# Batch 1 of a two-level Strassen layer: seven block sums and differences at other places of VectorE's order

## The chip, the cores and the metric

The kernel runs on one core of a Trainium2 chip. The metric is the device time of one execution in microseconds (us); several executions are timed and the median is taken. A profile of one execution comes with it. In it PE is TensorE (PEld its weight loads), DVE VectorE, ACT ScalarE, and SP the queue from which all transfers are issued. L12 is line 12 of the kernel.

## What is computed

Cross-attention between 512 tokens and 32 state rows, for 8 batches of 8 heads, gives 544 rows of 512 columns per batch; a two-layer network with a quick GELU runs over all of them.

```python
scores = scale * x @ state^T                # (8, 8, 512, 32)
xread  = softmax(scores) @ state
scores2 = scale * state @ x^T               # (8, 8, 32, 512)
sread  = softmax(scores2) @ x
attn   = concat([xread, sread], axis=2)     # (8, 8, 544, 64)
x = attn.transpose(0, 2, 1, 3).reshape(-1, 512)
h = x @ w_in                                # w_in  512 x 2048
out = (h * sigmoid(1.702 * h)) @ w_out      # w_out 2048 x 512
```

## The kernel before

The second layer, `g @ w_out`, is done with Strassen's method in Winograd's form: seven products of half-size blocks instead of eight, with sums on both sides. From batch 1 on five or more of the seven are themselves done in this way, so that each consists of seven small products. For the weights' side, a block t with quarters b11, b12, b21, b22 needs three *small sums* (t1, t2, t4), which are kept in DRAM and loaded before they are used, and a *third* (b22 - b12), which overwrites the block's own quarter b12. These are made once, in batch 1 at the latest, by VectorE. After the third, the sums can no longer be made from the block.

```python
    def T_of(t, x0, x1):
        nc.vector.tensor_tensor(out=t, in0=x0, in1=x1, op=ALU.subtract)

    def low_sums(t, rooms):                   # three instructions of 128x512
        b11, b12, b21, b22 = halves_of(t)
        t1, t2, t4 = rooms
        return [(T_of, v) for v in ((t1, b12, b11), (t2, b22, t1), (t4, b21, t2))]

    def low_third(t):                         # one instruction of 128x4x128
        _, b12, _, b22 = halves_of(t)
        T_of(b12, b22, b12)
```

One product of seven small ones. x, y, z are banks of PSUM; `add` is VectorE's, `copy` ScalarE's. `at(i)` puts in, after the i-th small product, first the product's own further work (`own`) and then what hangs on the hook of that name: `P5.4` is the hook behind P5's fourth small product.

```python
    def strassen_low(left, right, bank, R, at):
        ...
        product(x, a11, b11, True)
        nc.scalar.copy(y, x)
        at(1)
        product(z, s1, t1, True)
        nc.scalar.copy(c22, z)
        at(2)
        product(y, s2, t2)
        nc.scalar.copy(c12, y)
        at(3)
        product(x, a12, b21)
        nc.scalar.copy(c11, x)
        at(4)
        product(y, a21, t3)        # t3 is the third
        add(c22, y, c22)           # L697
        at(5)
        product(z, s4, b22)
        add(c12, z, c12)           # L697
        at(6)
        product(y, a22, t4)        # writes y again
        nc.scalar.copy(c21, y)
        at(7)
```

The products of batch 1, in order (key is 1):

```python
        product(bank(0), A_of(0, 0), B11, "P1")         # batch 1: P1 and P2 in one piece
        nc.scalar.copy(k1, bank(0))
        ...
            for i in range(3):
                sums1[i]()
                hook(f"S1.{i}")
            third_of(S1)
            product(bank(1), A_of(0, 1), B21, "P2")     # hooks P2a and P2b after its halves
            tt(osb, bank(1), k1)
        out(0, 0, osb)
        ...
        hook("P2")
        ...                                             # s4, sums2, third_of(S2) in P5's at()
        o, h0, h1 = low_banks()                         # o is bank_o[1]
        strassen_low(left_of(S1, *r), (b11, t3, b21, b22, *low_b), [h0, h1, o], p5, at)   # P5: T1
        low_load(6, 1)                                  # B22's kept sums, for P3
        hook("P5")
        ...
        lowly("P6", left_of(S2, q1, q2, q4), T2, low_a, banks, k2, own6)
        low_load(3, 0)
        ...
        lowly("P3", left12, B22, low_b, [h0, h1, o], p3, own3)
        ...
        hook("run")                                     # here low4_load: T4's kept sums back
        ...
        lowly("P7", left3, T3, low_a, [o, h0, h1], k3, {k + 1: steps4[k : k + 1] for k in range(4)})
        ...
        lowly("P4", left4, T4, low_parts(a4["low4"]), [o, h1, h0], k1, ...)
```

T4's small sums are made in a tile with the tag xT, of which there is one buffer. Before that, batch 2's exponentials e2 lie there, from which four transfers to DRAM (`squares`) read. Their issue hangs on P2b.

```python
    def away(k):
        room = apool.tile([P, NPR, S], FP32, tag="xT", name=f"away_{k}")
        return room.rearrange("p j t -> p (j t)")[:, : 3 * FC]

    def T4_sum(i):
        if i == 0:
            away4.append(away(4))
        fn, args = low_sums(T4, low_parts(away4[0]))[i]
        fn(*args)
        if i == 2:
            low_keep(4, away4[0])             # to DRAM

    def eT_out(b):
        for j in range(NPR):
            src = e2_room[b][Ns * j : Ns * (j + 1), :NG].rearrange("n g (i q) -> n g i q", i=SCH)
            nc.sync.dma_start(squares[:, :, :, j].rearrange("i n g q -> n g i q"), src)
```

Into the same hooks goes the attention of batch 2: its scores (att_blocks, att_s_max) at P2a, `att_s_norm` and `x_max` at P6.1, `x_sub` at P6.2, and so on.

Of the kernel before, what the change touches and what calls it, by code (L numbers as in the profile page):

```python
# [20 lines left out]
def kernel(  # L21
# [85 lines left out]
    T2, T4 = T24[:, :, 0], T24[:, :, 1]  # L107
# [24 lines left out]
    def load_state(b):  # L132
        stn[b] = apool.tile([P, NG, D], FP32, tag="stn", name=f"stn_{b}", bufs=2)
        for g in range(NG):
            nc.sync.dma_start(stn[b][:, g], st_v[b, g])
# [16 lines left out]
    def load_x_squares(b):  # L152
        xsq[b] = xpool.tile([P, NPR, S], FP32, tag="xn", name=f"xsq_{b}")
        for g in range(NG):
            for k in range(D // Ns):
                o = D * g + Ns * k
                dst = xsq[b][o : o + Ns].rearrange("p j (t a) -> p j t a", a=Ns)
                for j in range(NPR):
                    nc.sync.dma_start(dst[:, j], x_sq[b, g, k][:, j])
# [478 lines left out]
    T3 = w_out[:, :HF, HN:]  # L638
# [12 lines left out]
    def low_keep(k, src):  # L651
        nc.sync.dma_start(outside[k], src)
# [21 lines left out]
    def low_sums(t, rooms):  # L674
# [5 lines that stand above are left out]
    def low_third(t):  # L680
        _, b12, _, b22 = halves_of(t)
        T_of(b12, b22, b12)
# [346 lines left out]
    def parts_x(b):  # L1029

        a = A[b]
        t1, t2, t3, t4 = ([t] for t in a["T"])
        r11, r21, r22 = [a["aT"][:, 0, :QT]], [a["aT"][:, 1, :QT]], [a["aT"][:, 1, QT:]]

        def left(u):
            c = u // 2
            lo, hi = a["M", c], a["M", 2 + c]
            return [lo[:, 0]], [lo[:, 1]], [hi[:, 0]], [hi[:, 1]], [a["S1"][:, c]], [a["S2"][:, c]], [a["S4"][:, c]]

        return left, (r11, r21, r22, t1, t2, t3, t4)  # L1040
# [230 lines left out]
    B11, B12, B21, B22 = (w_out[:, HF * i : HF * (i + 1), HN * k : HN * (k + 1)] for i in range(2) for k in range(2))  # L1271
# [18 lines left out]
    def out_of(b):  # L1290
        return lambda r, n: out_x[b, r, :, n].rearrange("r q n -> q r n")
# [28 lines left out]
    def turns_of(*lists):  # L1320

        for step in zip(*lists):
            for fn, args in step:
                fn(*args)
# [147 lines left out]
    for b in range(1, B):  # L1472
        if b == 2:

            turns_of(low_sums(B11, low_b))
            low_keep(0, turn_rooms[1])
            low_third(B11)
        if b > 1:
            beside = [(turns_of, ([*low_sums(B21, low_a), (low_keep, (1, turn_rooms[0])), (low_third, (B21,))],))]
            ahead = {"P1.1": [(up_strassen(b, S, *parts_x(b), A[b]["sums"], beside if b == 2 else ()), ())]}  # L1480
        else:
            ahead = {
                "P2b": [(low_made, (2, T2, 0)), (low_third, (T2,))],
                "P5.4": [(T4_sum, (0,))],
                "P5.6": [(T4_sum, (1,))],
                "P6.2": [(T4_sum, (2,))],
                "P6.4": [(low_third, (B22,))],
                "P3.4": [(low_third, (T3,))],
                "P7.3": [(low_third, (T4,))],
            }  # L1490
            for u in range(NU - 1):
                ahead[f"S1.{u}"] = [(s3, (1, u, S))]
        if b + 1 < B:
            hooks = hooks_next(b + 1)
        else:

            steps, left, right = sr_sums()
            order = (
                ("P5.6", 2), ("P6.1", 3), ("P6.3", 6), ("P6.4", 7), ("P7.5", 8), ("P7.6", 9), ("P4.1", 16, 17), ("P4.5", 18, 19),
            )  # L1500
            hooks = {name: [steps[i] for i in n] for name, *n in order}
            hooks["P3.7"] = [(low_third, (T1,))]
            beside = steps[10:16] + [(low_third, (t,)) for t in (B11, B21, T2, T3, T4, B22)]
            ahead["P2.1"] = [steps[i] for i in (0, 1)]
            ahead["P2.3"] = [steps[i] for i in (4, 5)]
        for name, first in ahead.items():
            hooks[name] = first + hooks.get(name, [])
        a4 = {}

        at = hooks.setdefault("run", [])  # L1510
        k = 3 if b + 1 < B else 0
        at[k:k] = [(low4_load, (a4,))]
        strassen_two(b, out_of(b), hooks, a4)
        if b + 2 < B:
            load_state(b + 2)
            load_x_squares(b + 2)
# [35 lines left out]
```

## Time and profile before

| | before |
|---|---|
| median of three runs | 700.7 us (699.64 to 701.02) |
| span of the profiled execution | 699.1 us |
| TensorE busy | 684.5 us (98%) |
| VectorE busy | 571.5 us (82%) |
| ScalarE busy | 321.0 us (46%) |
| bytes moved | 87.41 MB, mean 125 GB/s |
| mean granted clock of TensorE | 0.997 |
| batch 1's second layer in the span | about 147 to 204 us |

The busy share of an engine is an average over the whole span. A matmul counts as busy for as long as it takes, also when TensorE's clock is throttled, and so a slow stretch doesn't show as idle time. The time at which an instruction starts, and in brackets the idle time of its engine before it with the event that ended it, is read from the timeline.

### The profile page before, as it was taken

What the parts mean: (1) busy time and instruction counts of PE and PEld (TensorE: products, weight loads), DVE (VectorE), ACT (ScalarE), POOL (GpSimd) and SP (SyncE); (2) the same over time, 40 slices, a digit from 0 to 9 for tenths busy, and PEclk for the clock granted to TensorE, in tenths of its full rate; (3) what the DMA queues carried; (4) which work ended last, traced back from release to release, by engine and by line L of the source; (5) the groups of instructions that cost most, each with busy time, mean ns of one, the idle gap of its engine ahead of it and who ended that gap; (6) DMA issues with size and microseconds to landing.
All of it is one profiled execution on the core that took longest, in us unless ns stands there. A gap on an engine that the chain in (4) does not pass through costs nothing.

```text
span 699.1 us, 13774 instructions
## 1 busy us (share of the span) xinstructions
PE 684.5 (98%) x5359; PEld 579.6 (83%) x5359; DVE 571.5 (82%) x1210; ACT 321.0 (46%) x704; POOL 0.8 (0%) x8
## 2 busy tenths in 40 slices
PE   8989999998999999999999999999999999999996
PEld 3433587776998899889988999889988998999995
DVE  6999998998898889697969886988778895887540
ACT  5688843223337523654355434653376236422420
POOL 0000000000000000000000000000000000000000
PEclk9999999999999999999999999999999999999999
DMA  8921337056525374436551664157433740251001
GB/s 232 368 72 58 122 121 183 8 189 181 175 68 140 106 241 138 80 91 212 151 110 31 190 211 113 20 139 234 138 53 106 241 137 16 74 155 50 11 2 31
DMA packets 106321, 87.41 MB, mean 125 GB/s; under 512 B 64784, under 2 KB 85776, under 8 KB 106256
## 3 DMA queue, kind: packets, MB, share of 16 engines
q1 hardware_dynamic: 106256, 86.53, 42.6%
q8 instruction: 43, 0.70, 0.4%
q14 instruction: 22, 0.18, 0.1%
HBM read 68.94 MB, written 17.56 MB: 124 GB/s over the span
## 4 chain that ended last, share of the span: by engine, by line
PE 90%; ACT 4%; DVE 2%; DMA 2%; SPq 1%; issue 0%; DVEq 0%
PE low L692 26%; PE o L1104 15%; PE o L692 14%; PE upx L1104 6%; PE h L547 4%; PE o L1371 4%; PE M L329 4%; PE down L1371 3%; PE o L589 2%; PE upw L1104 2%; PE down_up L547 2%; PE o L741 1%; PE o L329 1%; PE warm L127 1%; PE upx_sr L1104 1%; PE sr L518 1%
## 5 line engine op out<-in xcount | busy, mean ns | idle before, releaser
L692 PE MATMUL low<-w_out,g 128*128 128x128 f32 x416 | 54.3, 276 | 0.0
L692 PEld LDWEIGHTS low<-w_out,g 128*128 128x128 f32 x416 | 50.5, 192 | 4.5 <-issue 4.2
L1104 PE MATMUL o<-ta,M 128*128 128x256 f32 x192 | 49.9, 382 | 0.0
L1104 PE MATMUL upx<-aT,M 128*128 128x256 f32 x192 | 49.3, 379 | 0.0
L692 PE MATMUL low<-low,g 128*128 128x128 f32 x336 | 43.7, 277 | 0.2 <-DVE later L697 0.2
L692 PEld LDWEIGHTS low<-low,g 128*128 128x128 f32 x336 | 40.7, 194 | 0.3 <-DVE later L697 0.3
L1104 PEld LDWEIGHTS o<-ta,M 128*128 128x128 f32 x192 | 35.5, 190 | 6.0 <-ACT g L1150 1.6
L1104 PEld LDWEIGHTS upx<-aT,M 128*128 128x128 f32 x192 | 36.0, 190 | 4.6
L476 ACT COPY M<-M 128x512 f32<-128x512 f32 x59 | 30.7, 595 | 16.9 <-PE M L329 16.9
L692 PE MATMUL low<-sums,later 128*128 128x128 f32 x280 | 36.7, 279 | 0.0
L1110 ACT ACTIVATE g<-o 128x512 f32<-128x512 f32 (+1 forms) x56 | 31.3, 559 | 10.5 <-PE o L1104 10.5
L692 PEld LDWEIGHTS low<-sums,later 128*128 128x128 f32 x280 | 34.4, 196 | 0.1
L329 PE MATMUL M<-w_in,stT 64*32 64x512 f32 x472 | 32.6, 595 | 0.0
L1104 PE MATMUL o<-ta,ms 128*128 128x256 f32 x120 | 30.8, 379 | 0.0
L547 PE MATMUL h<-aT,M 128*128 128x512 f32 x64 | 28.7, 599 | 1.4 <-ACT M L476 1.4
L1150 ACT COPY g<-o 128x512 f32<-128x512 f32 (+1 forms) x28 | 15.5, 554 | 25.4 <-PE o L1104 25.4
L547 PEld LDWEIGHTS h<-aT,M 128*128 128x128 f32 x64 | 11.8, 190 | 18.3 <-issue 12.0
L1110 ACT ACTIVATE g<-g 128x512 f32<-128x512 f32 (+1 forms) x28 | 16.8, 600 | 20.8 <-DVE g L1113 20.8
L227 ACT ACTIVATE low<-low,edge 128x512 f32<-128x512 int32 x30 | 21.6, 718 | 8.7 <-DVE low L216 8.6
L1104 PEld LDWEIGHTS o<-ta,ms 128*128 128x128 f32 x120 | 22.8, 190 | 3.1
L1104 PE MATMUL o<-aT,m 128*128 128x256 f32 x96 | 24.6, 379 | 0.0
L692 PE MATMUL low<-low,later 128*128 128x128 f32 x168 | 22.5, 281 | 1.9 <-DVE spare_M L697 1.9
(290 smaller groups left out, 1646.7 us busy)
## 6 DMA issues: line engine op xcount, KB each, us to landing
low<-low SPq DMA_DIRECT2D x108, 256.0 KB, 3.6
low<-low SPq DMA_DIRECT2D x11, 768.0 KB, 4.3
later<-in_moe_w_out_dram SPq DMA_DIRECT2D x16, 512.0 KB, 3.5
w_out<-in_moe_w_in_dram SPq DMA_DIRECT2D x12, 512.0 KB, 5.6
xsq<-in_x_dram SPq DMA_DIRECT2D x96, 64.0 KB, 2.3
xn<-in_x_dram SPq DMA_DIRECT2D x12, 512.0 KB, 4.2
out_dram<-osb SPq DMA_DIRECT2D x15, 256.0 KB, 2.2
out_dram<-later SPq DMA_DIRECT2D x14, 256.0 KB, 2.1
```

The costliest lines, as they stand in the source:

```text
L127: nc.tensor.matmul(ps, zeros[:, :P], zeros, start=True, stop=True)
L227: nc.scalar.activation(out=sc.bitcast(FP32), in_=sc, func=AF.Relu, bias=edge[0], scale=-8.0)
L329: nc.tensor.matmul(ps[g][st], A[b]["stT"][rows, st], rhs(rows, j), start=True, stop=True)
L476: nc.scalar.copy(m[:, g], ps[g])
L518: nc.tensor.matmul(ps[st, g], e, v, start=(c == 0), stop=(c == SCH - 1),)
L547: nc.tensor.matmul(hps, lhs[i], rhs[i], start=(i == 0), stop=(i == n - 1))
L589: nc.tensor.matmul(ps[:, r], lhs[f][:, P * r : P * (r + 1)], rhs[:, f], start=(first and r == 0 and f == 0), stop=(f == HF - 1), skip_grou ...
L692: nc.tensor.matmul(ps, lhs[f], rhs[:, f], start=(first and f == 0), stop=(f == QF - 1), skip_group_check=True)
L1104: nc.tensor.matmul(ps[:, k], lhs[i][:, o : o + P], rhs[i], start=(first and k == 0 and i == 0), stop=(i == n - 1), skip_group_check=True,)
L1110: nc.scalar.activation(out=dst, in_=src, func=AF.Gelu_apprx_sigmoid)
L1150: nc.scalar.copy(c12, Y(u))
L1371: nc.tensor.matmul(ps7[name][:, HN * r : HN * (r + 1)], lhs[:, P * r : P * (r + 1)], rhs, start=(i == 0 and r == 0), stop=(i == HF - 1), s ...
```

## The change

It takes the same seven VectorE instructions of batch 1 to other places of that engine's order: the three small sums of T4 from P5.4, P5.6 and P6.2 to P6.1, P6.2 and P6.3, and the thirds of B22, T2, T3 and T4 to earlier or later hooks. The order that the data demand is kept: each third after its block's sums and before the fifth small product that uses it. The aim is that T4's sums come at a point where their room is free, and that what stands in their old places waits for nothing.

```diff
             ahead = {
-                "P2b": [(low_made, (2, T2, 0)), (low_third, (T2,))],
-                "P5.4": [(T4_sum, (0,))],
-                "P5.6": [(T4_sum, (1,))],
-                "P6.2": [(T4_sum, (2,))],
-                "P6.4": [(low_third, (B22,))],
-                "P3.4": [(low_third, (T3,))],
-                "P7.3": [(low_third, (T4,))],
+                "P2a": [(low_third, (B22,))],
+                "P2b": [(low_made, (2, T2, 0))],
+                "P2": [(low_third, (T2,))],
+                "P5.4": [(low_third, (T3,))],
+                "P6.1": [(T4_sum, (0,))],
+                "P6.2": [(T4_sum, (1,))],
+                "P6.3": [(T4_sum, (2,))],
+                "P3.4": [(low_third, (T4,))],
             }
```

What is listed here runs ahead of the attention's steps on the same hook. `low_made` makes T2's three small sums and sends them to DRAM.

## The prediction

> **What bounds the kernel now.** I read the page first. Its busy shares say TensorE, and the slices say that it is nearly never idle:
>
> ```profile
> PE 684.5 (98%) x5359; PEld 579.6 (83%) x5359; DVE 571.5 (82%) x1210; ACT 321.0 (46%) x704; POOL 0.8 (0%) x8
> PE   8989999998999999999999999999999999999996
> PE 90%; ACT 4%; DVE 2%; DMA 2%; SPq 1%; issue 0%; DVEq 0%
> ```
>
> TensorE is 98% busy and carries 90% of the chain that ended last. No arithmetic is added or removed here, so the only time to be had is TensorE's remaining idle time, plus matmuls that count as busy but run slowly. I therefore looked at where the chain leaves TensorE inside the second-layer products of batch 1 (147 to 204 us, the only stretch whose order changes). The timeline of TensorE (start, length, tile, count, in brackets the idle time before and who ended it) has two stalls between 160 us and 190 us and one small one at 196 us:
>
> ```profile
> 165.95 1.16 PE L692 MATMUL o<-low,spare_M 128*128 128x128 f32 x8 [0.59 <-DVE osb L748]
> 169.63 1.06 PE L692 MATMUL o<-sums,spare_M 128*128 128x128 f32 x8
> 172.59 1.70 PE L692 MATMUL low<-low,later 128*128 128x128 f32 x8 [1.91 <-DVE spare_M L697]
> 174.08 1.92 PE L692 MATMUL low<-sums,later 128*128 128x128 f32 x8
> 175.79 1.37 PE L692 MATMUL low<-low,g 128*128 128x128 f32 x8
> 180.57 1.06 PE L692 MATMUL o<-low,later 128*128 128x128 f32 x8
> 196.66 1.16 PE L692 MATMUL low<-low,g 128*128 128x128 f32 x8 [0.16 <-DVE later L697]
> ```
>
> In the kernel's terms these rows are: P5's second, sixth and seventh small product, P6's first, second and seventh, and P7's seventh. P5.7 waits 1.91 us for VectorE's addition after P5.5. A small product normally starts 0.89 us after the one before (P6.3 177.00, P6.4 177.89, P6.5 178.79), but P5.7, P6.1 and P6.2 need 1.49, 1.71 and 1.21. The granted clock, in half-microsecond windows of TensorE (window, length, busy with count, clock, DMA share, GB/s), says why:
>
> ```profile
> 172.50:173.00 0.50, 0.41 (x3) 1.00 0.66 254
> 173.00:173.50 0.50, 0.50 (x5) 0.53 0.05 16
> ...
> 176.00:176.50 0.50, 0.50 (x4) 0.56 1.10 426
> 176.50:177.00 0.50, 0.50 (x7) 1.00 1.04 426
> ```
>
> The clock is halved for some 3.5 us after the stall. In 4 us windows over the first 236 us it is below 1.00 only here. The page's clock row shows 9 throughout, so the dip is easy to miss. The stall thus costs 1.91 us and then 4.57 us for 24 matmuls that take 2.68 us elsewhere in the chain, another 1.89 us.
>
> Why was VectorE late? Its timeline:
>
> ```profile
> 163.27 1.42 DVE L1274 TENSOR_TENSOR low<-sums,low 128x512 f32<-128x512 f32 x2 [0.46 <-DVE low L1274]
> 164.61 0.68 DVE L1274 TENSOR_TENSOR sums<-sums 128x512 f32<-128x512 f32 x1
> 165.21 0.68 DVE L748 TENSOR_TENSOR osb<-o,g 128x512 f32<-128x512 f32 x1
> 168.82 0.69 DVE L748 TENSOR_TENSOR g<-later,g 128x512 f32<-128x512 f32 x1
> 171.64 0.69 DVE L1274 TENSOR_TENSOR away<-sums 128x512 f32<-128x512 f32 x1 [2.14 <-DMA squares<-e]
> 172.25 0.28 DVE L697 TENSOR_TENSOR spare_M<-low,spare_M 128x128 f32<-128x128 f32 x1
> ```
>
> The first of T4's small sums (away<-sums) writes into the room from which the four transfers squares<-e still read. The chain has the last issued at 167.74 and 3.78 us to its landing, at 171.52. VectorE stands 2.14 us before it, and the addition that TensorE needs (spare_M, L697) is behind it in VectorE's order, although P5.5's result was ready at about 168.73 + 1.06 = 169.79. The earlier stall has the same form: the third of T2 (sums<-sums) stands ahead of the osb addition, which has to empty the bank that P5.2 writes.
>
> **What the Trainium skill says.** "TensorE: Matmul & The Clock Gate", "Architectural detail", states that VectorE's queue is strict first-in-first-out: what waits at its head holds all behind it. The trace agrees, with the 2.14 us. The same page, "What's actually happening", describes a clock gate that goes to half rate after a free-running window of about 3.4 us with too little activity, and needs as long a busy window to open again. Here the clock did fall to 0.50, and for about 3.5 us; but an idle stretch of 1.9 us was enough, so a window that is only partly idle can do it. An idle 1.45 us (at 36 us) did not: the clock there stays 1.00.
>
> **The change part by part.** A third or sum of 128x512 costs VectorE 0.60 us from start to start when work follows (164.61 to 165.21), a 128x128 addition 0.20 (172.25 to 172.45). All seven instructions (three sums of T4, four thirds) are kept and only change place. No engine but VectorE has its order changed.
>
> *Third of B22, from P6.4 to P2a.* It comes after third_of(S1), which starts at 158.03 and leaves VectorE idle 0.64 us until the score transposes at 159.35, which wait for TensorE. The third takes 158.63 to 159.23: free, within 0.1 us.
>
> *Third of T2, behind the osb addition.* P2's product ends at 160.75 + 3.72 = 164.47 and T2's last small sum ends at 163.27 + 1.42 = 164.69, so osb can start at about 164.65, not 165.21, and P5.2 at 165.35 instead of 165.95. TensorE gains 0.60 us for the moment. VectorE's later work is unmoved: both still end at 165.81.
>
> *T4's sums away from P5.4, third of T3 there.* VectorE reaches this place at 168.82 + 0.60 = 169.42 as before, but the third of T3 waits for nothing and ends its turn at 170.02. P5.5 will be ready (168.13 + 1.06 = 169.19), so the L697 addition runs 170.02 to 170.30, and P5.7 starts near 170.35 instead of 172.59. TensorE is free for it at 169.03 + 0.89 = 169.92, so a wait of about 0.4 us remains. *Gain at P5.7: 2.24 us.*
>
> *Clock.* With an idle stretch of about 0.4 us (0.59 at 165 and 0.7 at 10 to 13 us left the clock at 1.00) I expect no dip. Products follow at 0.893 us: P6.3 at 170.35 + 3 x 0.893 = 173.03 instead of 177.00, P6.5 at 174.82, P6.7 at 176.60 instead of 180.57. *Gain at P6.7: 3.97 us.*
>
> *T4's sums at P6.1, P6.2, P6.3.* VectorE: s4 at 170.22, the L697 addition after P5.6 at 170.82, s4 at 171.02, free at 171.62. The room comes free at 171.52, and the first sum started 0.12 us after that, 171.64. So it now stands there just when the transfers end: no wait to speak of. Then, with the starts of the trace before, 2.36 us to the place after the second spare_M sum of P6.2 (173.85 to 176.21, the same instructions): 174.01 for the second sum, x_sub 174.61, third sum 175.22, free at 175.82. P6.5 is ready 1.16 us after its start (178.79, addition 179.95), hence at 175.98. VectorE is there 0.16 us early, the addition ends at 176.27, and P6.7 can start on time at 176.60, with 0.33 us to spare.
>
> *Third of T4, from P7.3 to P3.4.* It takes the place of T3's third, so nothing moves until P7.3; from there VectorE has 0.60 us less before the addition that P7.7 waited 0.16 us for. That wait goes too: VectorE 196.66 - 3.97 - 0.60 = 192.09, TensorE 196.50 - 3.97 = 192.53. *Gain: 0.16 us.*
>
> Sum: 2.24 + (3.97 - 2.24) + 0.16 = 4.13 us. After 197 us TensorE's timeline shows no stall up to the last first-layer products that I looked at (285 us), and VectorE idles there now and again (1.92 us at 242, 2.03 at 255, both for TensorE), so the rest should move earlier as a block. 700.7 - 4.1 = 696.6 us.
>
> **Rivals.** *The wait moves to P6.5.* If the four transfers land later, or the first T4 sum pays for its four transfer waits one after the other, all beyond 0.33 us goes straight to P6.7. For: T4's sums now stand before that addition with no spare time, and DMA engines are 90% or more busy from 166 to 172.6. Against: the transfers' issue follows ScalarE's exponentials, which nothing here moves. A slip of 1 us gives 697.3. *The clock dips anyway.* The idle time would be about 0.4 us and the gate's windows run freely; then 1.9 us are lost again: 698.5. *VectorE becomes the bound.* From 181.96 to 196.41 it has no idle time, so a TensorE that gains can run into it. Against: its own waits of 2.14, 1.85 and 0.24 us go too, with 0.60 us of work taken out, 4.83 us in all, more than TensorE's 4.13; but a stumble in the middle could leave only half the gain: 698.6. *The gain is handed back later*, at a transfer that doesn't come earlier: 700.7. Against: x, the kept sums and the state are loaded when buffers come free, and these move along.
>
> **Range and chances.** 696.6 us, with 695.5 to 698.6 for 8 in 10: the low end is the sum with half a microsecond of further small waits gone and the runs' scatter (699.64 to 701.02), the high end one of the second or third rival in full. Over 2% would need 14 us either way, and a stretch with 2.7 us of stalls and 1.9 us of slow clock holds no such gain. Nothing new is put in that could cost as much. So 0.985 within 2%, 0.01 faster, 0.005 slower.
>
> **What would show it.** Right: P5.2 starts near 165.35 with hardly a wait; the addition before P5.7 runs at about 170.0 behind a third of T3 (w_out<-w_out); P5.7's wait is 0.3 to 0.6 us; clock 1.00 from 172 to 177; away<-sums first at 171.6; P6.7 at about 176.6; batch 2's first-layer products (upx) start at 203.9 - 4.1 = 199.8. Wrong: a TensorE wait at P6.5 to P6.7 on L697, a halved clock after P5.7, or a later stage of batch 2 that starts where it did before.

## The result and the profile after

The changed kernel takes 697.18 us (median of six, 696.78 to 697.51) against 700.59 us for the kernel before (six, 699.64 to 701.62): a ratio of 0.9952, 95% interval 0.9939 to 0.9964. A second comparison gave 697.01 us and 0.9949 (0.9935 to 0.9964). The change brings about half a percent; 696.6 us had been predicted.

The page of the changed kernel, busy times and the chain by engine:

```profile
PE 682.9 (98%) x5357; PEld 578.0 (83%) x5359; DVE 571.6 (82%) x1210; ACT 321.0 (46%) x704; POOL 0.8 (0%) x8
PE 90%; DVE 5%; DMA 2%; ACT 1%; SPq 0%; issue 0%; DVEq 0%
```

The work is the same (VectorE 571.6 us against 571.5). TensorE's busy time fell by 1.6 us although it does the same matmuls (two records of them are missing in this trace). That is the time of the halved clock: P5.7, P6.1 and P6.2 took 4.41 us before (172.59 to 177.00), and take 2.78 us here (170.38 to 173.16). TensorE's timeline, of the small products in the prediction P5.2, P5.6, P5.7, P6.7 and P7.7:

```profile
165.37 1.16 PE L692 MATMUL o<-low,spare_M 128*128 128x128 f32 x8
169.04 1.06 PE L692 MATMUL o<-sums,spare_M 128*128 128x128 f32 x8
170.38 1.16 PE L692 MATMUL low<-low,later 128*128 128x128 f32 x8 [0.28 <-DVE spare_M L697]
176.74 1.06 PE L692 MATMUL o<-low,later 128*128 128x128 f32 x8
192.51 1.06 PE L692 MATMUL low<-low,g 128*128 128x128 f32 x8
```

Of the three stalls of before (0.59, 1.91, 0.16 us) only one, at P5.7, is left, and it is 0.28 us. P6.7 starts 3.83 us earlier than before (180.57), P7.7 4.15 us (196.66). The granted clock in the stretch where it was halved (window, length, busy with count, clock, DMA share, GB/s):

```profile
173.00:174.00 1.00, 1.00 (x11) 1.00 0.75 244
174.00:175.00 1.00, 1.00 (x11) 1.00 1.02 367
```

And VectorE's timeline, with the same places as before:

```profile
162.47 0.68 DVE L1274 TENSOR_TENSOR low<-sums 128x512 f32<-128x512 f32 x1
163.25 1.42 DVE L1274 TENSOR_TENSOR low<-sums,low 128x512 f32<-128x512 f32 x2
164.62 0.69 DVE L748 TENSOR_TENSOR osb<-o,g 128x512 f32<-128x512 f32 x1
169.44 0.68 DVE L1274 TENSOR_TENSOR w_out<-w_out 128x512 f32<-128x512 f32 x1
170.04 0.28 DVE L697 TENSOR_TENSOR spare_M<-low,spare_M 128x128 f32<-128x128 f32 x1
171.64 0.69 DVE L1274 TENSOR_TENSOR away<-sums 128x512 f32<-128x512 f32 x1
```

The third of T3 (w_out) stands where the first T4 sum waited 2.14 us. The addition for P5.7 runs at 170.04 instead of 172.25, and the T4 sum comes at 171.64 without any wait. One row was not expected: T2's second small sum starts 0.78 us after the first, where it took 1.14 (162.13 to 163.27). The section on the thirds comes back to it.

### The profile page after: what moved, and what is told of

Its sections match the earlier page's. It is cut to its first block, busy times and chain, and to the rows that moved or that the text cites. A ratio compares the mean times of both kernels' runs of the same rounds, so it can differ in the third digit from the quotient of the medians.

```text
span 695.1 us, 13772 instructions
## 1 busy us (share of the span) xinstructions
PE 682.9 (98%) x5357; PEld 578.0 (83%) x5359; DVE 571.6 (82%) x1210; ACT 321.0 (46%) x704; POOL 0.8 (0%) x8
## 4 chain that ended last, share of the span: by engine, by line
PE 90%; DVE 5%; DMA 2%; ACT 1%; SPq 0%; issue 0%; DVEq 0%
PE low L692 27%; PE o L1104 15%; PE o L692 15%; PE upx L1104 6%; PE h L547 4%; PE o L1371 4%; PE M L329 4%; PE down L1371 3%; PE o L589 2%; PE upw L1104 2%; PE down_up L547 2%; PE o L741 1%; PE sr L518 1%; PE upx_sr L1104 1%; DMA out_dram<-osb_sr 1%; PE o L329 1%
## 5 line engine op out<-in xcount | busy, mean ns | idle before, releaser
L692 PEld LDWEIGHTS o<-w_out,g 128*128 128x128 f32 x160 | 19.4, 192 | 5.0 <-issue 5.0
```

The source lines that it names most:

```text
L692: nc.tensor.matmul(ps, lhs[f], rhs[:, f], start=(first and f == 0), stop=(f == QF - 1), skip_group_check=True)
```

## The experiments

Each run is compared with the kernel before on the same chip. All 85 executions of the kernel before that stood beside the experiments fall into two groups by their mean granted clock: 37 under 0.998 with a median of 701.57 us (700.97 to 702.59), and 48 at 0.998 or more with 699.86 us (699.25 to 700.86). I call them "with the dip" and "without". Both profiles taken of the kernel before are of the first kind.

### T4's sums alone, and the thirds alone

The theory was that the first T4 sum, at the head of VectorE's order, waits for its room and holds up the addition that TensorE needs. The rival: VectorE is the bound, and the thirds' places carry a good part. Each half of the change was run without the other. The first:

```diff
-                "P5.4": [(T4_sum, (0,))],
-                "P5.6": [(T4_sum, (1,))],
-                "P6.2": [(T4_sum, (2,))],
+                "P6.1": [(T4_sum, (0,))],
+                "P6.2": [(T4_sum, (1,))],
+                "P6.3": [(T4_sum, (2,))],
```

> Only T4's three small sums move (P5.4, P5.6, P6.2 to P6.1, P6.2, P6.3); the four thirds stay where they were before. Theory A (the gain comes from the first T4 sum no longer standing at VectorE's head, waiting for the four transfers out of its room, with a TensorE stall of 1.91 us and a halved clock of 1.89 us behind it): P5.2 still waits near 0.6 us and starts at 165.95; the addition before P5.7 runs at about 169.5; P5.7 starts at its free time, 170.5, with hardly a wait; clock 1.00 from 172 to 177; P6.7 at 176.8 (before 180.57, after 176.74); P7.7 keeps its wait of about 0.2 us; about 3.7 us less than before, 696.9 us. Rival B (the thirds' places matter as much, since VectorE is the bound): P6.5's addition comes late behind the third of B22 and P6.7 waits 0.5 us or more; gain 2 to 3 us, 698 us.

Measured: 697.76 us against 701.1, ratio 0.9956 (0.9941 to 0.9971), no execution with the dip. TensorE's timeline of this run, P5.2, P5.7, P6.7 and P7.7:

```profile
165.88 1.16 PE L692 MATMUL o<-low,spare_M 128*128 128x128 f32 x8 [0.58 <-DVE osb L748]
170.45 1.06 PE L692 MATMUL low<-low,later 128*128 128x128 f32 x8
176.70 1.15 PE L692 MATMUL o<-low,later 128*128 128x128 f32 x8
192.89 1.16 PE L692 MATMUL low<-low,g 128*128 128x128 f32 x8 [0.15 <-DVE later L697]
```

The stall of 0.58 us before P5.2 and that of 0.15 us before P7.7 are still there, the long one is gone, and P6.7 is as early as in the whole change (176.74). So the T4 sums carry nearly all of it: by P7.7 3.77 us of the 4.15 us of the whole change. The third of T2 gains 0.5 us at P5.2, nearly all of which the third of T3 at P5.4 gives back at P5.7 (170.45 here, 170.38 in the whole change). The starts came as expected; the time is 0.9 us above the expected 696.9 us, which, like the prediction, took the halved clock as lost in every execution.

The second half:

```diff
-                "P2b": [(low_made, (2, T2, 0)), (low_third, (T2,))],
-                "P5.4": [(T4_sum, (0,))],
+                "P2a": [(low_third, (B22,))],
+                "P2b": [(low_made, (2, T2, 0))],
+                "P2": [(low_third, (T2,))],
+                "P5.4": [(low_third, (T3,)), (T4_sum, (0,))],
...
-                "P6.4": [(low_third, (B22,))],
-                "P3.4": [(low_third, (T3,))],
-                "P7.3": [(low_third, (T4,))],
+                "P3.4": [(low_third, (T4,))],
```

> Only the four thirds move, as in the changed kernel (the third of T3 stands at P5.4 ahead of the first T4 sum); T4's sums keep their old places P5.4, P5.6, P6.2. Theory A: P5.2 starts 0.6 us earlier, at 165.4, and hands it back: the first T4 sum still waits for the transfers until 171.6, P5.7 still starts at about 172.6 after an idle 2.5 us, the clock is halved again for about 3.5 us, P6.7 at 180.6; only the 0.16 us at P7.7 goes; 700.4 us, no difference that shows. Rival B (the thirds carry a good part of the gain): 697 to 699 us.

Measured: 698.85 us, ratio 0.9969 (0.996 to 0.9977), with no dip in 15 executions. My theory had expected 700.4 us, and missed by 1.5 us; the time is within the 697 to 699 us of the rival. VectorE's timeline:

```profile
169.67 0.68 DVE L1274 TENSOR_TENSOR w_out<-w_out 128x512 f32<-128x512 f32 x1
170.97 0.69 DVE L1274 TENSOR_TENSOR away<-sums 128x512 f32<-128x512 f32 x1 [0.62 <-DMA squares<-e]
171.57 0.28 DVE L697 TENSOR_TENSOR spare_M<-low,spare_M 128x128 f32<-128x128 f32 x1
```

The wait is still there as the theory had it, but the four transfers landed 2.81 us after the last was issued, by the chain, and not 3.78 us. The room came free earlier, and the thirds have something to do with it. That is not the rival's reason, a bound by VectorE; three runs in the section on the thirds look for the cause.

### Another room for T4's sums

If it is the wait for the room and not the work at P5.4, another room in the old order must do as well as the new order. The first two sums went into a buffer that was free at the time:

```diff
         if i == 0:
-            away4.append(away(4))
-        fn, args = low_sums(T4, low_parts(away4[0]))[i]
+            own = apool.tile([P, NG, S], FP32, tag="aT", name="own_4").rearrange("p g t -> p (g t)")
+            ...                       # t1 and t2 in own; t4, at P6.2, still in away(4)
-            low_keep(4, away4[0])
+            nc.sync.dma_start(outside[4][:, : 2 * FC], away4[0])
+            nc.sync.dma_start(outside[4][:, 2 * FC :], last)
```

> The order of the kernel before, but the first two T4 sums are written into another buffer (tag aT, free at that time), which no transfer reads; only the third one, at P6.2, uses the room that the transfers out of e2 read. One transfer to DRAM more. Theory A (it was the wait for the room, not the work at P5.4): the T4 sum at P5.4 runs at 169.4 without a wait, the addition before P5.7 at 170.0, P5.7 at 170.5, clock 1.00, P6.7 at 176.8; 696.9 us. Rival C (0.6 us of any work at P5.4 is what held TensorE up, or the transfers slow TensorE themselves): P5.7 well after 171 us, gain under 2 us.

Measured: 697.73 us, ratio 0.9955 (0.9939 to 0.9971). VectorE's and TensorE's timelines:

```profile
169.59 0.68 DVE L1274 TENSOR_TENSOR own<-sums 128x512 f32<-128x512 f32 x1
170.19 0.28 DVE L697 TENSOR_TENSOR spare_M<-low,spare_M 128x128 f32<-128x128 f32 x1
```

```profile
170.68 1.06 PE L692 MATMUL low<-low,later 128*128 128x128 f32 x8
```

The same 0.6 us of work stands at P5.4 as before and holds nobody up. The cause is the reuse of a buffer that transfers still read; a different buffer or a different order cures it equally well.

### Work for TensorE within the stall

The prediction read a loss of 1.89 us to the halved clock, and put 1.73 us of it into its sum of 4.13 us. To part that from the stall, the kernel before got 14 added matmuls between P5.6 and P5.7, which write a bank that nobody reads:

```diff
+            def warm_fill():
+                ps = att_ps([P, FC], "fill")[:, : 2 * P]
+                v = ident.bitcast(mybir.dt.bfloat16)
+                for _ in range(14):
+                    nc.tensor.matmul(ps, v[:, :P], v, start=True, stop=True)
-                "P5.6": [(T4_sum, (1,))],
+                "P5.6": [(T4_sum, (1,)), (warm_fill, ())],
```

> The kernel before with 14 added matmuls (bf16, 128x256, into a bank that nobody reads, operands from the identity) between P5.6 and P5.7, so that TensorE works through most of the stall. Theory A (the slow matmuls after the stall come from the clock gate, which the idle time closes): P5.7 still starts at about 172.6, since the addition is as late as before, but the clock stays 1.00, P5.7, P6.1 and P6.2 take 2.7 us instead of 4.57, P6.7 at 178.8; 1.8 us less than before, 698.8 us. Rival D (the three products are slow for another reason, such as transfers or VectorE on the same memory): they still take 4.6 us, 700.6 us. If the added matmuls themselves take longer than the stall, P5.7 starts later and the gain is smaller by so much.

TensorE's timeline of that run, the added matmuls, P5.7, P6.1 and P6.2:

```profile
170.57 1.69 PE L1486 MATMUL fill<-ident 128*128 128x256 bf16 x14
172.51 1.16 PE L692 MATMUL low<-low,later 128*128 128x128 f32 x8 [0.24 <-DVE spare_M L697]
173.50 1.06 PE L692 MATMUL low<-sums,later 128*128 128x128 f32 x8
174.39 1.06 PE L692 MATMUL low<-low,g 128*128 128x128 f32 x8
```

P5.7 is as late as before, but the three products take 2.78 us (172.51 to 175.29) instead of 4.41 (172.59 to 177.00), at a clock of 1.00, and P6.7 comes at 178.86 instead of 180.57. The difference, 1.63 us, is what the halved clock costs. So TensorE's idleness is what halves the clock, and neither the transfers nor VectorE, which run as before, slow these products. The time, though, was 700.6 us (14 executions, none with the dip), ratio 0.9999 (0.999 to 1.0009): no gain, where 698.8 us had been expected. The dip had been in the profile of the kernel before, but only in some of its executions, as the two groups show.

The kernel before was profiled again:

> The kernel before, unchanged, for a second profile. Half of 28 executions of it show a mean granted clock of 0.997 and take 701.33 to 702.59 us, the other half 0.998 to 1.0 and 699.47 to 700.86 us. Theory A2 (the halved clock after the stall at P5.7 comes in only some executions): if this execution is one of the quick half, P5.7 still waits (1.2 to 2 us) but the three products behind it take 2.7 us; if it is one of the others, 4.6 us as in the first profile.

It took 701.74 us, clock 0.997. The windows of its TensorE in which the halved clock begins:

```profile
173.00:174.00 1.00, 1.00 (x10) 0.85 0.07 25
174.00:175.00 1.00, 1.00 (x7) 0.50 0.10 18
```

In the first profile it fell at 173.03; here at 173.70, by the mean of 0.85 in the first window, although P5.7 started at nearly the same time (172.59 and 172.69). The Trainium skill, "TensorE: Matmul & The Clock Gate", "What's actually happening", says that the window over which activity is judged is 3413 ns long, runs freely and doesn't reset with the program. The two traces agree. The clock stays halved for 3.41 us in each, and falls once more at the end, when TensorE has no work left, at 698.68 in the first profile and at 699.34 here, by the mean clocks of 0.84 and 0.67. The first profile:

```profile
698.00:699.00 1.00, 0.00 (x0) 0.84 0.00 0
```

This one:

```profile
699.00:700.00 1.00, 0.00 (x0) 0.67 0.00 0
```

In both that is 525.65 us after the first fall, or 154 times 3413 ns. Every one of the 14 profiles shows a fall at the end, so its windows can be counted back from there, as an estimate with the page's 3413 ns. Each window in which TensorE idled 1.91 us or more ends with a fall (16 windows), and none with 1.88 us or less does, such as that with the 1.59 us of the thirds alone. In both profiles of the kernel before the whole stall at P5.7 lies within one window. If the windows fall anywhere with equal chance, that is to be expected in (3.41 - 1.91) / 3.41 = 0.44 of the executions, and 37 of 85 is 0.44. The phases of the other executions aren't recorded.

With five added matmuls in place of 14:

> As with the 14 added matmuls between P5.6 and P5.7, but 5 of them, about 0.6 us of work instead of 1.7. Theory A2 (14 of them kept the clock up in all executions, but were longer than the stall in many and held P5.7 up): 0.6 us is shorter than any stall seen, so P5.7 isn't held up; if 0.6 us of work in the stall is enough for the clock, all executions come at 700.0 us, where the quick half of the kernel before lies; if not, some still have 0.997 and 701.7 us, and the median lies between. Rival D (the fill changes nothing about the clock, and the two groups of times have another cause): two groups again, in equal parts, median 700.8 us.

700.33 us (13 executions), ratio 1.0002 (0.9994 to 1.0011). The two groups in equal parts, which rival D had expected, aren't there: 12 executions take 700.04 to 700.69 us. One of these shows 0.997, and the longest, 701.69 us, shows 0.998; whether either had the dip isn't known. In the profile of this run TensorE idles 1.36 us behind the five, and the clock stays 1.00 there:

```profile
172.49 1.16 PE L692 MATMUL low<-low,later 128*128 128x128 f32 x8 [1.36 <-DVE spare_M L697]
```

Both fills lie 0.5 to 0.7 us above the executions of the kernel before without the dip (699.86). I had put that to the fill being longer than the stall. In neither profile is it: P5.7 starts at 172.51 and 172.49, and was at 172.59 before. In both, TensorE waits once more at 250 us, for 0.39 and 0.55 us, where no other profile has a wait. That would be of the right size, but one execution of each doesn't show it, so where this half microsecond goes stays open.

### Why the thirds helped: T2's kept sums and the four transfers

T2's three small sums are sent to DRAM (768 KB) just ahead of the four transfers out of e2. In the next run the kernel before sent them behind:

```diff
-                "P2b": [(low_made, (2, T2, 0)), (low_third, (T2,))],
+                "P2b": [(turns_of, (low_sums(T2, low_a),)), (low_third, (T2,))],
+                "P2": [(low_keep, (2, turn_rooms[0]))],
```

> The kernel before, but T2's small sums (768 KB) are sent to DRAM behind the four transfers out of e2 and the first output instead of ahead of them; nothing else moves. Theory E (the four transfers land late, 3.8 us after the last is issued, because the kept sums are ahead of them on the same DMA engines): they land near 170.3, the wait at VectorE for T4's room falls from 2.14 to about 0.9 us, P5.7 starts at about 171.3, too short a stall to halve the clock; 698.6 us. Rival F (their 3.8 us is their own, with packets of 512 bytes): they land at 171.5 as before; 700.9 us.

699.02 us, ratio 0.9979 (0.9972 to 0.9987), no dip in 21 executions. From its chain and from VectorE's timeline:

```profile
167.84 2.76 DMA squares<-e
```

```profile
170.83 0.69 DVE L1274 TENSOR_TENSOR away<-sums 128x512 f32<-128x512 f32 x1 [1.24 <-DMA squares<-e]
```

2.76 us to the landing instead of 3.78. So one microsecond of the transfers' time, and 0.9 us of the stall, came from the 768 KB ahead of them. P5.7 waits 1.01 us instead of 1.91 and starts at 171.78. The Trainium skill, "DMA: Bandwidth & Descriptors", "Two DMAs through the same engine are not ordered", says that descriptors within one queue of one engine start in order, though they overlap. A large transfer issued shortly before could then hold back the next. The later landing agrees with that; when the four transfers began to move data isn't in the traces.

The thirds alone, profiled a second time:

> Only the four thirds move, a second profile. Theory E (with the thirds moved, T2's second small sum starts 0.78 us after the first instead of 1.14, so its kept sums are sent earlier against the four transfers, which then land earlier): first to second sum 0.78 us again, transfers 2.7 to 2.9 us after the last issue instead of 3.8, P5.7 1.6 us late at most, clock 1.00. Rival F (that profile was a stray): 1.14 us, 3.8 us, P5.7 at 172.6.

698.54 us. T2's first and second sum start at 162.11 and 162.89 (0.78 us), the four transfers land 2.95 us after the last issue, P5.7 starts at 171.75. So the first profile was no stray. Which of the thirds does it? That of B22 alone at P2a:

```diff
+                "P2a": [(low_third, (B22,))],
...
-                "P6.4": [(low_third, (B22,))],
```

> The kernel before with the third of B22 alone at P2a instead of P6.4. Theory E1 (this one instruction more ahead of T2's sums is what shortens the step from T2's first to its second sum): 0.78 us, the four transfers land about 1 us earlier, P5.7 at 171.7 instead of 172.6, clock mostly 1.00; 699 us. Rival E2 (it is the order of the third of T2 and the osb addition behind the sums): 1.14 us, transfers as before, P5.7 at 172.6, the clock halved in half of the executions; 700.7 us.

699.3 us, ratio 0.9985 (0.9975 to 0.9995), the dip in 2 of 19 executions. VectorE's timeline:

```profile
158.63 0.69 DVE L1274 TENSOR_TENSOR w_out<-w_out 128x512 f32<-128x512 f32 x1
162.01 0.68 DVE L1274 TENSOR_TENSOR low<-sums 128x512 f32<-128x512 f32 x1
162.79 1.42 DVE L1274 TENSOR_TENSOR low<-sums,low 128x512 f32<-128x512 f32 x2
170.47 0.69 DVE L1274 TENSOR_TENSOR away<-sums 128x512 f32<-128x512 f32 x1 [1.44 <-DMA squares<-e]
```

0.78 us between the sums, with the third of T2 where it was. The kept sums go out at 164.24 us, 1.25 us ahead of the first of the four transfers (165.49), in place of 0.92 (164.72 and 165.64), and the four land 2.77 us after the last issue. The rows of the transfer queue in this run:

```profile
164.24 0.34 SPq L652 DMA_DIRECT2D low<-low  x1
165.49 2.70 SPq L484 DMA_DIRECT2D squares<-e  x4
```

And in the kernel before:

```profile
164.72 0.34 SPq L652 DMA_DIRECT2D low<-low  x1
165.64 2.75 SPq L484 DMA_DIRECT2D squares<-e  x4
```

In the four profiles with the kept sums 0.92 to 0.94 us ahead, and VectorE waiting, the landing took 3.63 to 3.78 us; in the three with 1.25 to 1.31 us ahead 2.77 to 2.95. Why a third of a microsecond more saves as much as sending the 768 KB behind isn't shown.

In every profile without B22's third at P2a the step from T2's first to its second sum is 1.13 to 1.14 us, in every one with it 0.78 to 0.79. That the instruction does it is shown; by what means is not. It isn't that VectorE was idle before the score transposes: with the other room that idle time was 0.12 us, with the 14 added matmuls there was none, and the step was 1.14 both times.

### The wait that was left

At P5.7 the changed kernel still waits 0.28 us for the addition behind the third of T3. That third is needed only at P7.5 and was moved on by two hooks:

```diff
-                "P5.4": [(low_third, (T3,))],
+                "P5.6": [(low_third, (T3,))],
```

> The changed kernel with the third of T3 at P5.6 instead of P5.4. It should take away the rest of the wait at P5.7 (0.28 us idle, 0.45 us late): the addition before P5.7 at 169.6, P5.7 at its free time 169.95 instead of 170.38; VectorE then adds after P5.6, does s4 and the third of T3 by 171.6, when the room for T4's first sum comes free, so nothing is late further on; P6.7 at 176.3 instead of 176.74, about 0.4 us less than the changed kernel: 696.8 us. Rival B (VectorE is by now the bound): P6.5's addition comes no earlier than 176.1 and P6.7 not before 176.5, gain 0.2 us or less.

696.79 us, ratio to before 0.9948 (0.9935 to 0.9962). The changed kernel and this variant were then run side by side:

> The changed kernel, unchanged, beside the variant with the third of T3 at P5.6, on the same chip: 697.2 us, clock never under 0.998, since the wait at P5.7 of 0.3 us is too short to halve it. Rival (the first comparison was a lucky chip): 698 us or more, or some executions at 0.997.

> The changed kernel with the third of T3 at P5.6, a second time. Theory A: 0.4 us below the changed kernel of the same chip (P6.7 at 176.2 against 176.74), 696.8 us. Rival B (the difference of the first time, 696.79 against 697.18, was scatter): no difference.

The changed kernel: 697.01 us (696.79 to 698.07). The variant: 696.7 us (696.29 to 697.04), ratio to before 0.9943 (0.9929 to 0.9957). TensorE's timeline of the variant, P5.7, P6.7 and P7.7:

```profile
169.97 1.06 PE L692 MATMUL low<-low,later 128*128 128x128 f32 x8
176.22 1.12 PE L692 MATMUL o<-low,later 128*128 128x128 f32 x8
192.06 1.06 PE L692 MATMUL low<-low,g 128*128 128x128 f32 x8
```

No stall is left from P5 to P7. P7.7 starts at 192.06 against 192.57 in the changed kernel beside it. The traces show 0.5 us; the medians differ by 0.3 to 0.4 us both times, with ranges that overlap and intervals against before that do too. By the trace it is the best version, by the times only probably so.

## Why the prediction was right or wrong

- **What bounds it, and the cause of the stall: right.** The first T4 sum's wait for its room held up the addition, and with it TensorE. T4's sums moved alone, and another room in the old order, each take the stall away.
- **Third of B22 at P2a "free, within 0.1 us": not quite.** In this profile VectorE came to the place 0.46 us later (158.49 instead of 158.03), an offset that is there at 146 us already, so the transposes started 0.34 us later. It cost nothing because T2's second sum came 0.36 us sooner after the first than before, which I had not foreseen; B22's third itself is what shortens that step.
- **Third of T2, P5.2 at 165.35: right**, 165.37.
- **P5.7 near 170.35: right**, 170.38, with 0.28 us of idle time instead of about 0.4. **P6.7 at 176.60**: 176.74; the first product after a stall takes 1.00 us instead of 0.893, which I had left out. **T4's first sum at 171.64, the addition after P6.5 at 175.98**: 171.64 and 176.11. **P7.7 at 192.53**: 192.51. **Batch 2's first layer at 199.8**: 199.65.
- **The clock: mechanism right, size wrong.** This is the term of the sum that was mis-sized. The prediction put 1.73 us (3.97 - 2.24) into it, which one profile showed, as if lost in every execution. In an execution with the dip it is 1.63 us (4.41 - 2.78): a first product after a stall takes 1.00 us at full clock too, which also makes the 1.89 us that the prediction read too large. And it is lost in 37 of 85 executions: 0.44 x 1.63 = 0.71 us on the mean. The term was thus 1.0 us too large, yet the gain forecast, 4.13 us, lies only 0.6 to 0.7 us above the measured 3.41 and 3.53 us, because 0.3 to 0.4 us were gained elsewhere. That part of the closeness is luck.
- **What the traces account for.** P7.7 starts 4.15 us earlier (196.66 to 192.51), against an execution with the dip; without the 1.63 us this is 2.52 us. Against the executions without the dip (699.86) the changed kernel gains 2.7 to 2.85 us, so 0.2 to 0.3 us isn't located. The stretch behind P7.7 takes 502.4 to 503.4 us in the profiles. In nine of the 14 TensorE waits there once, for 0.16 to 0.63 us, mostly for a load of kept sums, each at one of four places; but two executions of the same kernel differ in it as well (the kernel before: none and 0.50 us), so single traces don't settle it.
- **Rivals.** The wait did not move to P6.5, the clock did not dip, VectorE did not become the bound, and nothing was handed back. But the reasoning against the first was too confident: I held the transfers' landing to be fixed by their issue. It moves by a microsecond with what is queued ahead of them, and how long before (3.78 to 2.76 us). In the changed kernel that did no harm: its first T4 sum found the room free at 171.64.
- **The thirds.** In the sum they had 0.16 us, plus what they let pass. Alone they bring 1.0 us against the executions without the dip (698.85 against 699.86). The prediction had no term for the larger part of that, the transfers' earlier landing: P5.7 starts at 171.91 and 171.75 instead of 172.59. In the whole change this is hidden, since VectorE gets to T4's first sum at 171.6 anyway. The two halves of the change therefore don't add up.

## What to carry to other kernels

A write into a reused buffer waits for the slowest transfer that still reads it (here 2.14 us), and in VectorE's order everything behind it waits too. Put such a write where the room is surely free, or give it another buffer, and set work without waits in its old place. Then look at what is queued just ahead of those transfers, because a large store that nobody awaits can delay a small one that somebody does (here by 1.0 us). And before a halved clock in one trace goes into a sum, look at the mean clock of every execution, together with its time: it tells roughly how often the loss is paid (here 37 of 85). It isn't a sharp measure, for the clock is also halved for up to 3.3 us at the very end, where TensorE has no work and nothing is lost; the changed kernel's 0.998 comes from there.

## What the runs showed that I had not expected

- TensorE's clock was halved for 3.41 us after an idle stretch of 1.91 us in 37 of 85 executions, which took 701.57 against 699.86 us. In the profiles it takes an idle 1.91 us within one window of 3.41 us; 1.88 us left it at 1.00. With stalls of 1.6 to 1.7 us (the thirds alone) it came in none of 15, with 1.0 us in none of 21. With 1.2 us (B22's third alone) it came in 2 of 19; these two took 3.0 us more than the median, so their stall may have been longer than that of the profile.
- Four transfers of 128 KB land 3.6 to 3.8 us after the last is issued with 768 KB sent 0.9 us ahead of the first, and 2.8 to 2.95 us after it with the 768 KB behind them or 1.25 to 1.31 us ahead.
- The third of B22, 3.4 us ahead of T2's first small sum, shortens the step to the second, dependent one from 1.14 to 0.78 us.
